# Attention over a pooled grid, then a mixture of adapters: the hidden activations made transposed, gates sent through DRAM, and a new run-out

## The chip, the cores and the metric

The kernel runs on one core of a Trainium2 chip. The core has five engines that this text speaks of: TensorE (PE in the profile, with its weight loads as PEld), VectorE (DVE), ScalarE (ACT), GpSimd (POOL) and SyncE (SP), which only issues transfers here. Transfers run on 16 DMA engines that all queues share. The metric is the device time of one execution in microseconds (us); the time of a kernel is the median of several runs.

## The reference

Four batches of 12,288 queries with 128 channels attend to keys and values that come from a grid, and each attended row then goes through the two best of eight small adapters.

```python
# attention; B, C, H, W = 4, 128, 384, 32, q has H*W rows a batch
kv_pool = kv.reshape(B, H // r, r, W // r, r, C).mean(axis=(2, 4))     # r = 4: 768 keys a batch
k = v = kv_pool.reshape(B, -1, C) @ w_sr
s = (q @ k.transpose(0, 2, 1)) / sqrt(C)
x = softmax(s) @ v                                                     # 49152 x 128 in all
# adapters: E = 8, rank 16
logits = x @ w_gate
top two of the eight logits, w = softmax over these two
delta = sum over the two of  w * ((x @ A[e]) @ B[e])
out = x + delta
```

## The kernel before

The 49,152 rows are worked in 96 chunks (NCH) of 512 rows (NTOK), 24 chunks to a batch. A chunk is four blocks (NS) of 128 rows. Two chunks form a pair, which shares the tiles of the gates.

A chunk c passes these steps, each named by its function:

- `scores(c, r)`, three times: two matmuls of 512 columns give the scores of 256 keys, and ScalarE's exponential writes them as `tt` (lines 284 and 285).
- `weigh(c, h)`, two halves: 24 matmuls with `tt` as weights give the attended rows, their gate logits and the sum of the exponentials, in the two banks `xps` (line 297).
- `normalise(c)`: VectorE's reciprocal, one multiply into `xn`, and four searches for the largest logits (lines 304, 308, 315).
- `gate(p)` and `gate_weights(p)`, once a pair: four small operations on GpSimd, a tanh on ScalarE, two more on GpSimd; the result `gw` has rows on partitions and, for each block, eight gates (lines 324 to 335).
- `transposed(cx, ch)`: TensorE turns the four blocks of `xn` of one chunk and the four blocks of `hg` of an older one into one bank, `t_ps` (line 352), and VectorE copies both out at once (line 361).
- `down(c)`: four matmuls of 128 columns with the transposed x as weights give h, rows on partitions (line 375). `apply_gate(c)`: VectorE multiplies h by the gates, spread over the 16 columns of each expert, into `hg` (line 380).
- `up(c)`: four matmuls with the transposed `hg` as weights give the adapters' sum (line 400). `give(c)`: VectorE adds `xn` (line 407), and SP sends 256 KB out (line 413).

The order of the work on every engine is the order of the program: it is written out by hand (`manual_schedule`), and each engine takes its own instructions in that order. The loop at line 551 works on several chunks in one iteration c: the scores of chunks c + 1 and c + 2, weigh and normalise of c - 1, the transposes of x of c - 2 and hg of c - 4, down and gate of c - 3, up and output of c - 6. On TensorE one iteration reads: scores, first half of weigh, scores, up, second half of weigh, transposes, scores, down.

TensorE's results stand in banks: two tiles of two banks for scores (`ps_s`), two banks for `xps`, one for `t_ps`, and one (`ps_h`, tag `hd`) that h and the adapters' sum use in turn. A step that writes a bank waits until the bank's last reader is done.

SP's transfers are issued in program order too, and a transfer that waits holds up those behind it. On SP stand the rows of kv for later batches (`load_row`, line 85, 512 KB each, planned by chunk in `plan`), the transposing loads of q (`load_q`, line 274, every fourth iteration, from a half-precision copy in DRAM that GpSimd's queue makes, `cast_q`, line 95), and the outputs. All are hardware-issued on one queue, which the profile calls q1; GpSimd's are on q0.

After the loop comes a run-out (lines 604 to 664): the last two chunks' weigh and everything that is left of the last six chunks, in an order of its own, with the scores' banks given back and used as single banks (`bank`, `fbank`). There `give` has two other forms: ScalarE copies and GpSimd adds, and two outputs leave on ScalarE's queue. At the end a flag (`bad`) decides whether a slow exact branch runs; it does not run here.

## Time and profile before

| | |
|---|---|
| time, median of 3 runs | 395.42 us (394.81 to 395.48) |
| profiled execution, its own time | 395.21 us |
| its span, first to last instruction | 393.4 us |
| granted TensorE clock, mean | 0.997 |
| busy: PE, DVE, ACT, POOL | 377.9, 323.4, 305.9, 206.9 us |
| transfers | 76.47 MB, 194 GB/s in the mean |

The page of a profile gives each engine's busy time and the chain of work that ended last, followed back from the last instruction, by engine and line. A group row reads: line, engine, operation, output and inputs, shapes, count, then busy time, mean duration of one, and the idle time of the engine before it with what ended that. A row of the timeline reads: start and length in us, engine, line, operation, and how many were merged. A row of stretches gives, for each engine, busy time and instructions, then the granted clock, the DMA engines' busy share and GB/s. Matmuls are pipelined, so their durations overlap, and the distance between starts is what one costs.

### The profile page before, as it was taken

What the parts mean: (1) busy time and instruction counts of PE and PEld (TensorE: products, weight loads), DVE (VectorE), ACT (ScalarE), POOL (GpSimd) and SP (SyncE); (2) the same over time, 40 slices, a digit from 0 to 9 for tenths busy, and PEclk for the clock granted to TensorE, in tenths of its full rate; (3) what the DMA queues carried; (4) which work ended last, traced back from release to release, by engine and by line L of the source; (5) the groups of instructions that cost most, each with busy time, mean ns of one, the idle gap of its engine ahead of it and who ended that gap; (6) DMA issues with size and microseconds to landing.
All of it is one profiled execution on the core that took longest, in us unless ns stands there. A gap on an engine that the chain in (4) does not pass through costs nothing.

```text
span 393.4 us, 11525 instructions
## 1 busy us (share of the span) xinstructions
PE 377.9 (96%) x4589; PEld 301.2 (77%) x4589; DVE 323.4 (82%) x911; ACT 305.9 (78%) x387; POOL 206.9 (53%) x389
## 2 busy tenths in 40 slices
PE   4989999999999999999999999999999999999993
PEld 1457768888887887888878888888788888878882
DVE  3776777888888889888888888888888888888984
ACT  1558888878888888887877888888878877877863
POOL 1011598895688666563487666573442332322353
PEclk9999999999999999999999999999999999999998
DMA  8989997998898899298997998275678583222124
GB/s 255 393 279 167 358 262 229 275 218 218 258 211 234 256 164 266 83 211 246 238 238 225 241 237 211 92 166 130 135 92 205 136 188 102 88 82 83 55 86 160
DMA packets 69784, 76.47 MB, mean 194 GB/s; under 512 B 49664, under 2 KB 49920, under 8 KB 69376
## 3 DMA queue, kind: packets, MB, share of 16 engines
q1 hardware_dynamic: 67264, 63.45, 55.8%
q0 software_dynamic: 704, 11.54, 16.9%
q10 hardware_dynamic: 1760, 0.73, 0.7%
q8 instruction: 36, 0.59, 0.6%
q14 instruction: 20, 0.16, 0.1%
HBM read 50.53 MB, written 36.70 MB: 222 GB/s over the span
## 4 chain that ended last, share of the span: by engine, by line
PE 93%; ACT 2%; DMA 1%; POOL 1%; DVE 1%; issue 0%; ACTq 0%; POOLq 0%
PE xps L297 34%; PE sg L284 31%; PE t_ps L352 11%; PE d_ps L400 5%; PE h_ps L375 5%; PE w_ps L495 2%; PE v_ps L173 1%; DMA w_gate_sb<-in_moe_w_gate_dram 1%; ACT tt L285 1%; PE k_ps L198 1%; PE kp_ps L165 1%; ACT qT L481 0%; PE t_ps L477 0%; ACT xh L359 0%; POOL osb L411 0%
## 5 line engine op out<-in xcount | busy, mean ns | idle before, releaser
L285 ACT ACTIVATE tt<-sg 128x1024 f16<-128x1024 f32 x288 | 281.3, 1024 | 57.2 <-PE sg L284 56.8
L284 PE MATMUL sg<-qT,kfT 128*128 128x512 f16 x576 | 171.0, 379 | 1.3 <-ACT tt L285 1.0
L297 PEld LDWEIGHTS <-tt 128*128 128x128 f16 x2304 | 152.6, 112 | 22.1 <-DVE xn L308 0.7
L297 PE MATMUL xps<-vext,tt 128*128 128x137 f16 x2304 | 169.4, 223 | 0.0
L407 DVE TENSOR_TENSOR osb<-d_ps,xn 128x512 f32<-128x512 f32 x90 | 62.3, 692 | 35.3 <-PE d_ps L400 35.2
L324 POOL TENSOR_TENSOR arg<-xn,top 128x64 f32<-128x64 f32 x47 | 14.9, 317 | 121.6 <-DVE top L315 116.5
L308 DVE TENSOR_TENSOR xn<-xps,rinv_all 128x548 f32<-128x548 f32 x96 | 70.0, 729 | 3.3
L380 DVE TENSOR_TENSOR hg<-h_ps,gw 128x512 bf16<-128x512 f32 x93 | 63.2, 679 | 2.4 <-PE h_ps L375 2.4
L149 POOL TENSOR_TENSOR kvt<-kvt 128x1024 f32<-128x1024 f32 x27 | 63.9, 2368 | 1.3 <-PE sg L284 1.1
L361 DVE COPY xh<-t_ps 128x1024 bf16<-128x1024 bf16 (+1 forms) x93 | 62.5, 672 | 0.0
L284 PEld LDWEIGHTS <-kfT 128*128 128x128 f16 x576 | 45.0, 98 | 3.6 <-issue 2.1
L375 PEld LDWEIGHTS <-xh 128*128 128x128 bf16 x384 | 29.3, 98 | 21.5
L400 PEld LDWEIGHTS <-xh 128*128 128x128 bf16 x384 | 29.1, 98 | 21.5 <-ACT xh L359 0.6
L315 DVE MAX8 top<-xn 128x8 f32<-128x8 f32 x384 | 35.9, 156 | 3.3
L352 PE MATMUL t_ps<-id_bf,hg 128*128 128x128 bf16 x376 | 36.3, 219 | 0.5 <-ACT xh L359 0.5
L352 PE MATMUL t_ps<-id_bf,xn 128*128 128x128 bf16 x376 | 36.3, 219 | 0.0
L400 PE MATMUL d_ps<-b_bf,xh 128*128 128x128 bf16 x368 | 35.6, 219 | 0.5 <-ACT xh L359 0.5
L375 PE MATMUL h_ps<-a_bf,xh 128*128 128x128 bf16 x372 | 35.9, 219 | 0.0
L352 PEld LDWEIGHTS <-xn 128*128 128x128 bf16 x384 | 26.4, 98 | 0.7 <-DVE xn L308 0.4
L352 PEld LDWEIGHTS <-hg 128*128 128x128 bf16 x384 | 25.3, 98 | 0.9 <-DVE hg L380 0.8
L334 POOL TENSOR_SCALAR th<-th 128x64 f32<-128x64 f32 x48 | 18.0, 375 | 13.7 <-ACT th L332 13.5
L304 DVE RECIPROCAL rinv_all<-xps 128x4 f32<-128x4 f32 x96 | 17.5, 183 | 7.5 <-PE xps L297 5.0
(112 smaller groups left out, 240.2 us busy)
## 6 DMA issues: line engine op xcount, KB each, us to landing
kvt<-in_kv_dram SPq DMA_DIRECT2D x48, 512.0 KB, 6.1
out_dram<-osb SPq DMA_DIRECT2D x94, 256.0 KB, 3.0
q_h<-in_q_dram POOLq DMA_DIRECT2D x22, 512.0 KB, 7.1
q<-in_q_dram SPq DMA_DIRECT2D x2, 1024.0 KB, 9.9
out_dram<-osb ACTq DMA_DIRECT2D x2, 256.0 KB, 3.5
qT<-q_h SPq DMA_TRANSPOSE x22, 8.4
w_in<-in_w_sr_dram ACTq DMA_DIRECT2D x1, 64.0 KB, 1.8
a_f<-in_moe_A_dram ACTq DMA_DIRECT2D x1, 64.0 KB, 10.5
```

The costliest lines, as they stand in the source:

```text
L149: eng.tensor_tensor(v[:, 0], v[:, 0], v[:, d], op=ALU.add)
L284: mm(sg[:, k], kfT[b][:, j * P:(j + 1) * P], qc, start=True, stop=True)
L285: nc.scalar.activation(tt[c][:, 2 * r:2 * r + 2], sg, AF.Exp, bias=0.0, scale=scale)
L297: mm(o, tt[c][:, j, rows], vext[b][:, j, 0:VW], start=(j == 0 and s % 2 == 0), stop=(j == NJ - 1 and s % 2 == 1), skip_group_check=True)
L308: nc.vector.tensor_tensor(xn[c].rearrange("p (b s) v -> p b s v", b=2), xv, ri.rearrange("p (b s) -> p b s", b=2).unsqueeze(3).broadcast_t ...
L315: nc.vector.max(gin[c // 2][:, (c % 2) * NS + s], xn[c][:, s, C:C + E])
L352: mm(t_ps[:, k, s], src, id_bf, is_transpose=True, start=(i == 0), stop=(i == len(todo) - 1), skip_group_check=True)
L361: nc.vector.tensor_copy(xh[:, lo:hi_], t_ps[:, lo:hi_])
L375: mm(hps[c][:, s], xT[c][:, s], a_bf, start=(s == 0), stop=(s == NS - 1))
L380: nc.vector.tensor_tensor(hg[c].rearrange("p s (e r) -> p (s e) r", r=RK), hps[c].rearrange("p s (e r) -> p (s e) r", r=RK), g.rearrange(" ...
L400: mm(dps[c][:, s], hgT[c][:, s], b_bf, start=(s == 0 and fresh), stop=(s == NS - 1), skip_group_check=True)
L407: nc.vector.tensor_tensor(osb, dps[c], xn[c][:, :, 0:C], op=ALU.add)
```

## The change

Four things change.

1. **h is made transposed.** In the loop, `gated_hidden(c)` takes `a_bf` as the weights and the transposed x of a chunk as 512 moving columns: one matmul gives h with the adapters' columns on partitions. VectorE multiplies it by gates of the same layout, and the result is already what `up` wants as weights. So `hg` is not transposed for these chunks.
2. **The gates come transposed over DRAM.** `gw` is now in half precision. Once a pair, TensorE transposes it (64 rows of 128) into the bank `t_ps`; VectorE copies it out, SP stores it in DRAM (`g_h`, 16 KB), and `load_gates` reads it back so that each expert's row stands on its 16 partitions (256 KB in SBUF). This holds for the first 90 chunks (`OWN`); the last six keep the old way.
3. **The lags change.** gated_hidden works on chunk c - 6, up and output on c - 7. The evacuations of x and of the gates are separate copies, the output has 6 buffers instead of 8.
4. **The run-out is new.** Banks are taken and given back in another order, ScalarE copies most results out (`take`), GpSimd adds four of them, all outputs leave on SP, and the last chunk is worked in two halves. The check that sets `bad` comes last.

Beside these, the last two kv rows are loaded as two halves each, and the four `kpT` tiles are slices of one, which saves three transfers in the branch that does not run.

```diff
+    g_h = qdram.tile([NCH // 2, E, 2 * NS, P], F16, name="g_h")
...
-        gw[p] = small.tile([P, 2 * NS, E], FP32, tag="gw", name="gw")
+        gw[p] = small.tile([P, 2 * NS, E], F16, tag="gw", name="gw")
...
+    def transposed(cx, cg=NCH, p=NCH):
+        t_ps = ps_t.tile([P, 2, NS, P], BF16, tag="tp", name="t_ps")
+        hi = xn[cx].bitcast(U16)[:, :, 1:2 * C:2].bitcast(BF16)
+        more = chunk_ok(cg) or p < NCH
+        for s in range(NS):
+            mm(t_ps[:, 0, s], hi[:, s], id_bf, is_transpose=True,
+               start=(s == 0), stop=(s == NS - 1 and not more), skip_group_check=True)
+
+        def second():
+            if chunk_ok(cg):
+                for s in range(NS):
+                    mm(t_ps[:, 1, s], hg[cg][:, s], id_bf, is_transpose=True,
+                       start=False, stop=(s == NS - 1), skip_group_check=True)
+            elif p < NCH:
+                mm(t_ps[0:2 * NS * E, 1, 0].bitcast(F16), gw[p].rearrange("p s e -> p (s e)"),
+                   id_h, is_transpose=True, start=False, stop=True, skip_group_check=True)
 
         def evacuate(act=False):
...
+            if p < NCH:
+                g_sb = small.tile([2 * NS * E, P], F16, tag="gt", name="g_sb")
+                copy(g_sb, t_ps[0:2 * NS * E, 1, 0].bitcast(F16))
+                nc.sync.dma_start(g_h[p].rearrange("e s t -> s e t"), g_sb)
+            xT[cx] = run.tile([P, NS, P], BF16, tag="xt", name="xt", bufs=5)
+            copy(xT[cx], t_ps[:, 0])
...
+    def load_gates(p):
+        gE[p] = run.tile([P, 2 * NS, P], F16, tag="ge", name="ge", bufs=3)
+        nc.sync.dma_start(
+            gE[p].rearrange("p s t -> p (s t)"),
+            g_h[p].rearrange("e s t -> e (s t)").unsqueeze(1).broadcast_to([E, RK, 2 * NS * P]))
+
+    def gated_hidden(c):
+        h_ps = mtile([P, NS, P], name="h_ps")
+        mm(h_ps, a_bf, xT[c], start=True, stop=True)
+        hgT[c] = run.tile([P, NS, P], BF16, tag="ht", name="ht", bufs=3)
+        nc.vector.tensor_tensor(hgT[c], h_ps, gE[c // 2][:, (c % 2) * NS:(c % 2 + 1) * NS],
+                                op=ALU.mult)
...
         weigh(c - 1, 0)
+        if c == NCH - 2:
+            down(c - 4, stile("h_ps")[:, 0])
+            apply_gate(c - 4)
         next_scores()
-        if chunk_ok(c - 6):
-            up(c - 6)
-            give(c - 6)
+        if chunk_ok(c - 7):
+            up(c - 7)
+            give(c - 7)
+        if c % 2 == 0 and 0 <= (c - 4) // 2 < OWN // 2:
+            load_gates((c - 4) // 2)
         weigh(c - 1, 1)
...
-        evacuate = transposed(c - 2, c - 4)
+        pair = (c - 3) // 2
+        second, evacuate = transposed(
+            c - 2, c - 4 if c - 4 >= OWN else NCH, pair if c % 2 and 0 <= pair < OWN // 2 else NCH)
         next_scores()
...
-        if chunk_ok(c - 3):
-            down(c - 3)
+        if chunk_ok(c - 6):
+            gated_hidden(c - 6)
+        second()
+        if c == NCH - 2:
+            down(c - 3, stile("h_ps")[:, 0])
             apply_gate(c - 3)
         evacuate(c == NCH - 2)
...
     gate_weights(q_ - 1, nc.gpsimd)
+    y4 = ps_x.tile([P, 2, 512], FP32, tag="x", name="y4")
+    weigh(n - 1, 0, y4)
+    gated_hidden(n - 6)
+    up(n - 7, bank(0))
+    give(n - 7)
     weigh(n - 1, 1)
...
+    turn(high(n), 0, NS, bank(0), xT, n)
+    gate_args(n, 0, NS, nc.vector, top5, arg5, msk5)
+    gate_tanh(0, NS, arg5)
...
+    for c, o in ((n - 6, o6), (n - 5, o0), (n - 4, o1), (n - 3, o2)):
+        add(c, o, nc.gpsimd)
+        put(c, o)
+        if c == n - 4:
+            put(n - 2, o3)
     tail_ok()
...
+    up(n - 1, mtile([P, NTOK], name="d4"))
+    give(n - 1)
...
+    put(n, o5)
+    all_ok(bank(1))
```

Here `take(c)` is ScalarE's copy of the adapters' sum, `add` the addition of `xn` in place, `put` the output's transfer, `turn` a transpose with its evacuation, and n is the last chunk, 95.

More of the change, by code (lines that the diff above doesn't have):

```diff
@@ new lines, in turn @@
+    def turn(src, lo, hi, bank_, store, key, act=True):
+        t_ps = bank_.bitcast(BF16)[:, 0:(hi - lo) * P].rearrange("p (s c) -> p s c", c=P)
+        for s in range(lo, hi):
+            mm(t_ps[:, s - lo], src[:, s], id_bf, is_transpose=True,
+               start=(s == lo), stop=(s == hi - 1), skip_group_check=True)
+        if key not in store:
+            x_or_h = ("xt", 5) if store is xT else ("ht", 3)
+            store[key] = run.tile([P, NS, P], BF16, tag=x_or_h[0], name="xr", bufs=x_or_h[1])
+        if act:
+            nc.scalar.activation(store[key][:, lo:hi], t_ps, AF.Copy)
+        else:
+            nc.vector.tensor_copy(store[key][:, lo:hi], t_ps)
@@ new lines, in high, with hidden @@
+    def high(c):
+        return xn[c].bitcast(U16)[:, :, 1:2 * C:2].bitcast(BF16)
+    def hidden(c, lo, hi, bank_):
+        hb = as_tokens(bank_)[:, 0:hi - lo]
+        for s in range(lo, hi):
+            mm(hb[:, s - lo], xT[c][:, s], a_bf, start=(s == lo), stop=(s == hi - 1))
+        return hb
+    n = NCH - 1
+    q_ = n // 2
+    top = small.tile([P, 2 * NS, 8], FP32, tag="top", name="top")
+    top4, top5 = top[:, 0:NS], top[:, NS:2 * NS]
+    pair = xpool.tile([P, 2 * NS, VW], FP32, tag="xn", name="xn")
```

223 lines of the change are left out of this document (133 added, 90 removed).

## The prediction

> **What bounds the kernel now.** I read the page first: busy shares, then the chain that ended last, which names the engine whose time is the kernel's time.
>
> ```profile
> PE 377.9 (96%) x4589; PEld 301.2 (77%) x4589; DVE 323.4 (82%) x911; ACT 305.9 (78%) x387; POOL 206.9 (53%) x389
> ...
> PE 93%; ACT 2%; DMA 1%; POOL 1%; DVE 1%; issue 0%; ACTq 0%; POOLq 0%
> PE xps L297 34%; PE sg L284 31%; PE t_ps L352 11%; PE d_ps L400 5%; PE h_ps L375 5%; PE w_ps L495 2%; PE v_ps L173 1%; DMA w_gate_sb<-in_moe_w_gate_dram 1%; ACT tt L285 1%; PE k_ps L198 1%; PE kp_ps L165 1%; ACT qT L481 0%; PE t_ps L477 0%; ACT xh L359 0%; POOL osb L411 0%
> ```
>
> The chain is TensorE for 93% of the span, and transposes (L352) are 11% of it. Next the groups by line and shape, and then one iteration of the loop in order of time, TensorE and then VectorE.
>
> ```profile
> L352 PE MATMUL t_ps<-id_bf,hg 128*128 128x128 bf16 x376 | 36.3, 219 | 0.5 <-ACT xh L359 0.5
> L361 DVE COPY xh<-t_ps 128x512 bf16<-128x512 bf16 x3 | 1.2, 415 | 0.0
> L409 ACT ACTIVATE osb<-d_ps 128x512 f32<-128x512 f32 x2 | 1.2, 597 | 0.6 <-PE d_ps L400 0.6
> ```
>
> ```profile
> 203.55 0.39 PE L352 MATMUL t_ps<-id_bf,xn 128*128 128x128 bf16 x4
> 203.77 0.39 PE L352 MATMUL t_ps<-id_bf,hg 128*128 128x128 bf16 x4
> 204.00 0.59 PE L284 MATMUL sg<-qT,kfT 128*128 128x512 f16 x2
> 204.43 0.39 PE L375 MATMUL h_ps<-a_bf,xh 128*128 128x128 bf16 x4
> 204.65 0.59 PE L284 MATMUL sg<-qT,kfT 128*128 128x512 f16 x2
> ...
> 206.24 0.39 PE L400 MATMUL d_ps<-b_bf,xh 128*128 128x128 bf16 x4
> 206.46 0.88 PE L297 MATMUL xps<-vext,tt 128*128 128x137 f16 x12
> 207.18 0.39 PE L352 MATMUL t_ps<-id_bf,xn 128*128 128x128 bf16 x4
> ```
>
> ```profile
> 203.75 0.18 DVE L304 RECIPROCAL rinv_all<-xps 128x4 f32<-128x4 f32 x1
> 203.97 0.73 DVE L308 TENSOR_TENSOR xn<-xps,rinv_all 128x548 f32<-128x548 f32 x1
> 204.73 0.37 DVE L315 MAX8 top<-xn 128x8 f32<-128x8 f32 x4
> 205.03 0.67 DVE L380 TENSOR_TENSOR hg<-h_ps,gw 128x512 bf16<-128x512 f32 x1
> 205.61 0.68 DVE L361 COPY xh<-t_ps 128x1024 bf16<-128x1024 bf16 x1
> 206.66 0.69 DVE L407 TENSOR_TENSOR osb<-d_ps,xn 128x512 f32<-128x512 f32 x1 [0.37 <-PE d_ps L400]
> ```
>
> Starts, not durations, give the price on TensorE, since its matmuls overlap. One iteration is 207.18 - 203.55 = 3.63 us; one starts with the scores at 204.65, so the others at 201.02 and 211.91. The four transposes of hg take 204.00 - 203.77 = 0.23 (0.056 each), one 512-column matmul (204.43 - 204.00) / 2 = 0.215, the four of h_ps 204.65 - 204.43 = 0.22. VectorE works 3.32 us of the 3.63.
>
> **The change, part by part.** *Transposes of hg* go for 90 of the 96 chunks (the last six keep the old way): 90 x 0.225 = 20.2 us. *h as one 512-column matmul* instead of four of 128: 0.215 against 0.22, nothing. *A transpose of the gates* for each of 45 pairs, with 128 moving columns: 45 x 0.056 = 2.5 us. TensorE's balance is -17.7 us, all on the chain, if nothing else becomes late. The iteration falls to about 3.43 us.
>
> *VectorE.* The evacuation shrinks from 0.68 to 0.415 (the 128x512 row); the multiply by gates keeps its size (0.67); a copy of 64x128 gates comes every second iteration, at most the 0.42 of the 128x512 row. The sum is 0.18 + 0.73 + 0.37 + 0.67 + 0.42 + 0.21 + 0.69 = 3.27, under 3.43. *ScalarE* needs three exponentials and half a tanh:
>
> ```profile
> 201.00 1.94 ACT L285 ACTIVATE tt<-sg 128x1024 f16<-128x1024 f32 x2 [0.74 <-PE sg L284]
> 202.83 0.26 ACT L332 ACTIVATE th<-arg 128x64 f32<-128x64 f32 x1
> 203.63 0.32 POOL L335 TENSOR_TENSOR gw<-th,msk 128x64 f32<-128x64 f32 x1
> ```
>
> 3 x 0.97 + 0.13 = 3.0, also under. The gate transpose runs where h_ps ended (204.65 here) and POOL's gw is ready at 203.95: TensorE does not wait for it. The banks of xps come free later relative to need: normalise ends at 204.70 and the next weigh starts at 204.65 + 0.43 = 205.08; this slack of 0.38 falls by the 0.2 saved, to 0.15 or so, still positive. These parts I cost at nothing; if a cover is gone, each lost 0.1 us costs 9 us over 92 iterations.
>
> *The way over DRAM.* The path is: copy of gates to SBUF at an odd iteration's end, store, load behind it on SP, multiply in the iteration after next. The load cannot be issued before the store has landed, and in every second pair it stands on SP behind a transposing load of q (L274) and an output.
>
> ```profile
> kvt<-in_kv_dram SPq DMA_DIRECT2D x30, 512.0 KB, 5.5
> out_dram<-osb SPq DMA_DIRECT2D x50, 256.0 KB, 4.9
> ...
> qT<-q_h SPq DMA_TRANSPOSE x13, 8.8
> ```
>
> ```profile
> DMA to landing us min/median/max: 5.0/8.8/12.2
> ```
>
> ```profile
> DMA to landing us min/median/max: 3.8/8.1/9.9
> ```
>
> The issue table of 47 to 235 us, and the landing times of q's transposing loads there and (7 loads) from 235 to 345 us. SP's own rows:
>
> ```profile
> 48.55 1.86 SPq L274 DMA_TRANSPOSE qT<-q_h  x1
> ...
> 212.69 4.38 SPq L274 DMA_TRANSPOSE qT<-q_h  x1
> 217.16 1.65 SPq L413 DMA_DIRECT2D out_dram<-osb  x2
> ...
> 227.27 3.05 SPq L274 DMA_TRANSPOSE qT<-q_h  x1
> ```
>
> The price of one 256 KB transfer in the DMA engines' time comes from the quiet stretch 335 to 373 us, where only ten outputs run (second column of the queue row MB, third share of 38 us):
>
> ```profile
> q1 hardware_dynamic: 1516, 2.75, 18.8%
> ...
> out_dram<-osb SPq DMA_DIRECT2D x10, 256.0 KB, 2.0
> ```
>
> 0.188 x 38 / 10 = 0.71 us. A gate load moves as many bytes, so 0.71 is its lower bound; the upper is 1.42, that of an input row of 512 KB at this rate, because reads from DRAM land slower than writes (kv 5.5 against 4.9 us median). I take 0.71, as it has the output's bytes. The store (16 KB) counts 0.1.
>
> The budget from the start S of an iteration with a q load: two periods, then 205.03 - 201.02 = 4.0 us into the third until VectorE multiplies, then 0.3 us of slack until the next up needs the result (now 206.24 - 205.70 = 0.54, less the 0.2 saved). With key and value work the period up to 230 us is (227.27 - 48.55) / 48 - 0.2 = 3.52, later 3.43. So 11.3 and 11.15 us. Spent of it: q's load starts 0.8 after S (212.69 against 211.91); now the gate store stands ahead of it on SP, ready only 1.5 after S (VectorE's multiply ends 4.7 after the iteration before began, 0.2 for the copy, less 3.43), which I cost at nothing where the load is late, because there the queue is full anyway (4.38 us to issue one), and at 1.1 us more at the upper end. Output and gate load follow at 0.71 each. The gates are late when q's load takes over 11.3 - 0.8 - 1.4 = 9.1 us (8.95 later). Spreading the upper half of the landings evenly, 8.8 to 12.2: mean excess 3.1² / 2 / 3.4 = 1.41, times 6.5 loads = 9.2 us. Later, 8.1 to 9.9: 0.95² / 2 / 1.8 = 0.25, times 3.5 = 0.9. A late multiply holds VectorE and then TensorE's up, so it is lost in full: +10.1 us. With 1.1 us more spent the first half gives some 20, the second 4: upper end +24. The lower end is 0, if the queue drains better.
>
> *SP and POOL.* Stores and loads are 90 more issues on SP, which waits for the store's landing with outputs and kv rows queued behind it; outputs have 6 buffers, 20 us of cover. POOL loses nothing in the loop. The split of two kv rows is two more issues of 0.5 us, hidden; kp_keep works in the untaken branch only.
>
> *The run-out.* It carries more: up is one chunk later, h three chunks, so 0.22 x 3 of TensorE work moves behind the loop, and ScalarE evacuates 12 times 0.6 us after weigh of chunk 94. Against that the last transfer no longer leaves on ACT's queue:
>
> ```profile
> 377.51 1.60 PE L297 MATMUL xps<-vext,tt 128*128 128x137 f16 x24
> ...
> 387.79 0.69 DVE L407 TENSOR_TENSOR osb<-d_ps,xn 128x512 f32<-128x512 f32 x1 [0.17 <-PE d_ps L400]
> ```
>
> ```profile
> out_dram<-osb ACTq DMA_DIRECT2D x2, 256.0 KB, 3.5
> ```
>
> From that weigh's end (379.1) to the span's end, 393.4, is 14.3 us now: the last addition ends at 388.5, its output lands 3.5 later and 1.4 more pass. In the new order ScalarE is what I find last: 0.6 until its first copy, 8.3 of copies and tanh in one row, 1.6 for the final up and addition, an output from SP at the 2.0 us of the quiet stretch, and the 1.4: 13.9. With the 0.6 that the loop hands over, net +0.2, counted as 0, bounds -1.5 to +1.5.
>
> **Sum.** Profiled run 395.2 (span 393.4 + 1.8 around it): 395.2 - 17.7 + 10.1 + 0 = 387.6. The median of the runs is 0.2 above: 387.8.
>
> **The rivals.**
> *A, no lateness.* Landings shrink because DMA has idle time after 235 us. 395.4 - 17.7 = 377.7. For it: half the landings are already short enough; against: 9 us is passed often.
>
> *B, slower: the DMA engines become the bound up to 235 us.*
>
> ```profile
> 47.00:108.00 61.00, 60.03 (x745) 48.34 (x743) 49.94 (x143) 50.53 (x66) 48.61 (x74) 1.00 0.93 249
> 108.00:171.00 63.00, 63.00 (x796) 51.25 (x795) 54.09 (x152) 51.95 (x65) 46.28 (x71) 1.00 0.84 205
> 171.00:235.00 64.00, 64.00 (x806) 51.93 (x805) 55.19 (x161) 52.74 (x67) 38.83 (x73) 1.00 0.94 233
> ```
>
> The column before the last is the DMA share: 0.93 x 61 + 0.84 x 63 + 0.94 x 64 = 169.8 us of 188. The faster loop would have 188 - 50 x 0.2 = 178 for it, and 25 pairs come on top. At 1.42 + 0.1 each that is 38, so 208 us of work: the stretch lasts 208, and 395.4 - 17.7 + 30 = 408. It decides once a pair costs over (178 + 17.7 - 169.8) / 25 = 1.04 us; at 0.81 it gives 390. That point lies 0.23 above my price and 0.48 below the upper one, and outputs that land at 4.9 us in this stretch against 2.0 in the quiet one show how much queue there is already; but a share that counts overlapping packets twice overstates the work. So a third of the chance.
>
> The Trainium skill, "DMA: Bandwidth & Descriptors", section "Why a DMA increments its semaphore by 16 and not by 1", says that a transfer is spread over the largest number of engines, up to 16, that divides the outermost dimension of both sides. The gate load's source has 8 experts outermost, so by that rule 8 engines carry it at twice the time, and B's upper price would hold: 408 by it, 388 by mine. The trace of before has no transfer of that shape and cannot show it.
>
> *C, some wait eats the gain without DMA* (VectorE or the xps banks, 0.19 us in each of 92 iterations): 395.4 - 17.7 + 17.5 = 395.2. Against it: VectorE's 0.37 us of idle.
>
> **How the numbers follow.** Forecast 0.36 (382 to 394), A 0.23, B 0.34, C 0.07. About 0.2% is what a measurement can tell from no change, 394.6 to 396.2. Faster 0.36 + 0.23 + 0.02 = 0.61, same 0.05, slower 0.34. The forecast is the likeliest, 387.8; the 8 in 10 range goes from A to just short of B's upper price, 378 to 405.
>
> **What would show it.** Right: L352 loses the hg group, TensorE idles before up (L400), released by VectorE's hgT multiply that itself waits for the DMA of the gates, mostly in iterations with a q load before 235 us; a period of about 3.43 elsewhere. A: no such wait. B: the wait comes in nearly every pair before 235 us and the DMA share there is near 1. Wrong in another way: a wait of TensorE for normalise, or a run-out more than 1.5 us longer.

## The result, and the profile after

The changed kernel takes 454.0 us (median of four executions, 448.1 to 461.3) against 395.1 us: a ratio of 1.144, with an interval of 1.133 to 1.155. The prediction was 387.8 us, with a range of 378 to 405. It missed both the sign and the range. An execution over 1.5% above the quickest of its kernel counts as slow: one of these four (461.3 us, which the ratio leaves out), three of the four each of e7, e11, e13 and e16, and the profiled ones of e4, e8, e9, e11, e13 and e16.

The page of the changed kernel, its busy line, two rows of the slices and the chain:

```profile
PE 389.3 (86%) x4008; PEld 277.4 (61%) x4008; DVE 308.4 (68%) x957; ACT 311.9 (69%) x393; POOL 206.3 (46%) x393
...
PEclk9999988997999699899989789999999999999998
DMA  8989797967979989869889967986798696532314
...
PE 55%; DMA 30%; DVE 7%; SPq 3%; issue 2%; ACT 1%; DVEq 0%
PE xps L306 21%; PE sg L293 19%; DMA ge<-g_h 15%; DMA g_h<-g_sb 13%; PE d_ps L432 4%; PE t_ps L353 3%; PE h_ps L396 3%; SPq L93 2%; DVE ht L398 2%; DMA kvt<-in_kv_dram 2%; DVE xn L317 1%; PE t_ps L362 1%; PE v_ps L182 1%; SPq L451 1%; PE w_ps L536 1%
```

TensorE has 581 instructions fewer than before, and the chain has left it: 55% instead of 93%. The two transfers of the gates are 28% of the chain, the load (ge<-g_h) 15% and the store in front of it (g_h<-g_sb) 13%. The list of waits (total, times, longest) says who stood for them, first the engines, then SP's queue:

```profile
DVE ht L398 <- DMA ge<-g_h: 58.3, 22, 11.6
PE d_ps L432 <- DVE ht L398: 47.1, 18, 11.3
```

```profile
SPq L389 <- DMA g_h<-g_sb: 66.9, 22, 8.1
```

VectorE waits 58.3 us for gates, TensorE's `up` then waits 47.1 us for VectorE, and the load itself stands on SP, 22 times, until the store has landed, 66.9 us in all. The stretches, in the columns of the prediction (the last three are clock, DMA share, GB/s):

```profile
47.00:108.00 61.00, 42.93 (x396) 28.97 (x394) 29.73 (x94) 33.16 (x41) 38.38 (x48) 0.89 0.85 214
108.00:171.00 63.00, 54.83 (x579) 39.46 (x578) 42.11 (x134) 44.60 (x57) 36.14 (x63) 0.95 0.87 211
171.00:235.00 64.00, 58.36 (x608) 42.23 (x606) 45.44 (x146) 46.84 (x60) 30.98 (x58) 0.95 0.87 215
```

Before, the same stretches had DMA shares of 0.93, 0.84 and 0.94. With 45 more stores and 45 more loads on the queue, two of the three are lower, so by this share the DMA engines are not the bound (a kernel that runs late also asks for its transfers later). One wait for gates, rows of VectorE, TensorE and SP in order of time, with rows between them left out:

```profile
149.20 0.69 DVE L398 TENSOR_TENSOR ht<-h_ps,ge 128x512 bf16<-128x512 f32 x1 [7.26 <-DMA ge<-g_h]
149.95 0.61 PE L432 MATMUL d_ps<-b_bf,ht 128*128 128x128 bf16 x4 [6.94 <-DVE ht L398]
150.35 1.59 PE L306 MATMUL xps<-vext,tt 128*128 128x137 f16 x12
151.04 0.60 SPq L389 DMA_DIRECT2D ge<-g_h  x1
```

Behind a wait of 7 us, twelve matmuls of `weigh` take 1.59 us where the rows of before had 0.88. This long wait is paid a second time: the granted clock is 0.50 from 149.95 to 153.60 us, and such places pull the clocks of the stretches down to 0.89 and 0.95. (The Trainium skill, "TensorE: Matmul & The Clock Gate", Part 1, says that an idle window of about 3.4 us brings the clock to half; the trace agrees on the half, 0.50 behind a wait of 6.94 us, and these rows don't show how long the window is.)

The landing times follow from the semaphore updates in the trace. These are the transfers that belong to the wait at 149.20:

```
issue    queue  transfer          landed   after
132.27   SP     store of gates    140.48    8.2
132.98   SP     transposing q     146.64   13.7
133.77   POOL   cast of q         146.40   12.6
140.50   SP     load of gates     149.11    8.6     issued 0.02 after the store landed
```

8.2 and 8.6 us, one after the other. The multiply was due at 141.9. Counted in the same way over the pairs up to 240 us, a store takes 5.5 us to land in the median and the load behind it 4.7; from 383 us on, where little else moves, 1.8 and 3.6. The longest wait of all, 11.6 us, has another shape: its store landed after 4.2 us, SP was then busy for 3.4 us more with the issue of an output, and the load took 13.9 us. In both places a transposing load of q and a cast of q move at the same time, and these land after 13.7 and 12.6 us in the first, 18.4 and 17.1 in the second (before, the longest q load took 12.2). No run changes that overlap, so its share is open.

### The profile page after: what moved, and what is told of

It is laid out like the page before. It is cut to its first block, busy times and chain, and to the rows that moved or that the text cites. A ratio compares the mean times of both kernels' runs of the same rounds, so it can differ in the third digit from the quotient of the medians.

```text
span 452.5 us, 10659 instructions
## 1 busy us (share of the span) xinstructions
PE 389.3 (86%) x4008; PEld 277.4 (61%) x4008; DVE 308.4 (68%) x957; ACT 311.9 (69%) x393; POOL 206.3 (46%) x393
## 4 chain that ended last, share of the span: by engine, by line
PE 55%; DMA 30%; DVE 7%; SPq 3%; issue 2%; ACT 1%; DVEq 0%
PE xps L306 21%; PE sg L293 19%; DMA ge<-g_h 15%; DMA g_h<-g_sb 13%; PE d_ps L432 4%; PE t_ps L353 3%; PE h_ps L396 3%; SPq L93 2%; DVE ht L398 2%; DMA kvt<-in_kv_dram 2%; DVE xn L317 1%; PE t_ps L362 1%; PE v_ps L182 1%; SPq L451 1%; PE w_ps L536 1%
## 5 line engine op out<-in xcount | busy, mean ns | idle before, releaser
L294 ACT ACTIVATE tt<-sg 128x1024 f16<-128x1024 f32 x288 | 285.7, 1025 | 99.6 <-PE sg L293 98.9
L293 PE MATMUL sg<-qT,kfT 128*128 128x512 f16 x576 | 175.9, 389 | 1.4 <-ACT tt L294 1.0
L398 DVE TENSOR_TENSOR ht<-h_ps,ge 128x512 bf16<-128x512 f32 x90 | 61.3, 681 | 60.0 <-DMA ge<-g_h 58.3
L432 PE MATMUL d_ps<-b_bf,ht 128*128 128x128 bf16 x352 | 35.2, 224 | 47.2 <-DVE ht L398 47.1
L432 PEld LDWEIGHTS <-ht 128*128 128x128 bf16 x368 | 26.5, 99 | 74.8 <-DVE ht L398 59.8
L293 PEld LDWEIGHTS <-kfT 128*128 128x128 f16 x576 | 46.0, 99 | 18.4 <-issue 2.2
L370 DVE COPY xt<-t_ps 128x512 bf16<-128x512 bf16 x92 | 37.8, 411 | 0.0
L396 PE MATMUL h_ps<-xt,a_bf 128*128 128x512 bf16 x90 | 35.4, 393 | 0.3 <-DVE osb L446 0.2
L336 POOL TENSOR_SCALAR msk<-msk 128x64 f32<-128x64 f32 x47 | 17.5, 373 | 4.2
L362 PEld LDWEIGHTS <-gw 128*64 128x64 f16 x45 | 4.9, 108 | 21.5 <-issue 18.4
L344 POOL TENSOR_TENSOR gw<-th,msk 128x64 f16<-128x64 f32 x47 | 15.1, 322 | 3.9
```

The costliest lines, as they stand in the source:

```text
L293: mm(sg[:, k], kfT[b][:, j * P:(j + 1) * P], qc, start=True, stop=True)
L294: nc.scalar.activation(tt[c][:, 2 * r:2 * r + 2], sg, AF.Exp, bias=0.0, scale=scale)
L370: nc.vector.tensor_copy(dst, src)
L396: mm(h_ps, a_bf, xT[c], start=True, stop=True)
L398: nc.vector.tensor_tensor(hgT[c], h_ps, gE[c // 2][:, (c % 2) * NS:(c % 2 + 1) * NS], op=ALU.mult)
L432: mm(dps[c][:, s], hgT[c][:, s], b_bf, start=(s == 0 and fresh), stop=(s == NS - 1), skip_group_check=True)
```

## The experiments

Times in us below are medians. Where differences are worked out, each kernel stands as its ratio times 395.4.

**Without the transfers (e1).** Is the whole loss the gates' way over DRAM?

```diff
-                nc.sync.dma_start(g_h[p].rearrange("e s t -> s e t"), g_sb)
...
-        gE[p] = run.tile([P, 2 * NS, P], F16, tag="ge", name="ge", bufs=3)
-        nc.sync.dma_start(gE[p]..., g_h[p]...)
+        gE[p] = g_one                     # a constant tile
```

> The changed kernel without the store and the load of the gates: every chunk of the loop is multiplied by a constant 0.5 instead of its gates, so the output is not the reference's; all other work, the gates' transpose and copy too, stays. If the whole loss comes with these transfers, the 17.7 us of TensorE come out: 376 to 380 us, a granted clock near 1. If the loop or the run-out lost time by themselves (VectorE, the banks of xps), it stays above 390.

393.1, ratio 0.995 [0.991, 0.999]. The transfers cost some 59 us. But 393 is far above the 377.7 that the prediction gives without lateness: something else in the loop or the run-out is dearer than I had it. (The constant makes the output another than the reference's.)

**What the gate transpose costs (e5).** In e1's steady part the iterations take 3.40 and 3.68 us in turn, and only the second kind has the gate transpose. TensorE's rows in e1 around one, and the group of its weight loads:

```profile
203.32 0.38 PE L394 MATMUL h_ps<-xt,a_bf 128*128 128x512 bf16 x1
203.63 0.24 PE L364 MATMUL t_ps<-id_h,gw 128*64 128x128 f16 x1
203.81 0.60 PE L295 MATMUL sg<-qT,kfT 128*128 128x512 f16 x2
...
L364 PEld LDWEIGHTS <-gw 128*64 128x64 f16 x45 | 4.8, 106 | 21.6 <-issue 15.2 <-POOL gw L346 5.5 <-POOL sq L228 0.8
```

From h_ps to the scores is 0.49 us, where 0.215 for h_ps and 0.056 for the transpose make 0.27. The difference is around the load of weights, 64 columns wide where all others in the loop are 128. The experiment pads it with zeros:

```diff
-        gw[p] = small.tile([P, 2 * NS, E], F16, tag="gw", name="gw")
+        gw[p] = gws[p % 3][:, 0:2 * NS]          # gws: [P, 4 * NS, E], set to zero once
...
-                mm(t_ps[0:2 * NS * E, 1, 0].bitcast(F16), gw[p].rearrange("p s e -> p (s e)"),
+                mm(t_ps[:, 1, 0].bitcast(F16), gws[p % 3].rearrange("p s e -> p (s e)"),
```

> The kernel of e1 (no gates sent or fetched, the multiplication by a constant, so the output is not the reference's), with one thing changed: the gates stand in a block of 128 columns of which 64 are zero, so that the gate transpose on TensorE loads 128 columns of weights as its neighbours do, and not 64. In e1 the iterations without the gate transpose take 3.40 us and those with it 3.68 us, 0.28 us for one transpose where I had put 0.056 us. Theory narrow: it is the load of 64 columns that is not hidden behind the matmuls before it (its row shows 0.34 us of idle time per load, its neighbours 0.07 us or less); then the odd iterations fall to 3.46 us, 45 x 0.22 = 9.9 us go, and the kernel takes about 383 us (380 to 386). Theory wait: what costs is that the transpose waits for GpSimd's product, or that it stands by itself in the middle of other work; then the odd iterations stay at 3.6 to 3.7 us and the time at 392 to 394 us. The Trainium skill, TensorE: Matmul & The Clock Gate, section Weight-path perf modes, says that the fast weight load is taken when the number of weights is 128 and the type is not FP32; it speaks for the first theory.

383.7, ratio 0.969 [0.967, 0.972], 10 us less than e1 for a wider block of zeros. The same place in e5:

```profile
199.65 0.38 PE L398 MATMUL h_ps<-xt,a_bf 128*128 128x512 bf16 x1
199.86 0.22 PE L368 MATMUL t_ps<-id_h,gws 128*128 128x128 f16 x1
199.92 0.59 PE L299 MATMUL sg<-qT,kfT 128*128 128x512 f16 x2
```

0.27 us: the transpose costs 0.06 as predicted, once its weights are 128 wide. The trace agrees with the rule of the Trainium skill ("TensorE: Matmul & The Clock Gate", "Weight-path perf modes") that the expectation names, as far as the time goes: 0.28 us with 64 columns, 0.06 with 128.

**The load without the store's wait (e2).** The same bytes move, but the load reads a constant, the same 16 KB each time (and the output is another), and so waits for no store.

```diff
-            g_h[p].rearrange("e s t -> e (s t)")...
+            g_c[0].rearrange("e s t -> e (s t)")...      # written once, at the start
```

> The same stores and loads, but the loads read a constant that was stored once at the start, so no load waits for a store; the output is not the reference's, because the gates are constant. Theory 1 (two landings in a row: a store that lands behind rows of kv, and a load that SP holds until then): 380 to 400 us, and TensorE's wait for the gates falls from some 60 us to under 20. Theory 2 (the gate transfers take so much of the DMA engines that everything is late): above 430 us, since all the traffic is still there.

428.2, ratio 1.083 [1.074, 1.091]. Waiting for the store is worth some 24 us; 35 remain without it.

```profile
DVE ht L402 <- DMA ge<-g_c: 29.6, 13, 8.3
```

VectorE still waits, for loads that wait for nobody. The DMA shares of the three stretches are 1.02, 0.87 and 0.88 here, hardly above the changed kernel's in the last two, though SP stands for no store.

**The traffic by itself (e7), and over 16 engines (e12).** e7 is e2 with a product that reads a constant tile: the loads run and nobody wants them. e12 moves the same bytes in another order. (Both have two buffers for the gates instead of three.)

```diff
# e7, against e2
-        nc.vector.tensor_tensor(hgT[c], h_ps, gE[c // 2][...], op=ALU.mult)
+        nc.vector.tensor_tensor(hgT[c], h_ps, g_two[...], op=ALU.mult)
# e12, against e7: rank outermost in the load, one run per row in the store
-            g_c[0].rearrange("e s t -> e (s t)").unsqueeze(1).broadcast_to([E, RK, 2 * NS * P]))
+            g_c[0].rearrange("e s t -> e (s t)").unsqueeze(0).broadcast_to([RK, E, 2 * NS * P]))
-                nc.sync.dma_start(g_h[p].rearrange("e s t -> s e t"), g_sb)
+                nc.sync.dma_start(g_h[p].rearrange("e s t -> (e s) t"), g_sb)
```

> The traffic of e2 (a store and a broadcast load per pair, the load from a constant that is written once, so that it waits for no store), but the multiplication reads a constant tile: nobody waits for the loads any more, and the output is not the reference's. e1 without traffic took 393.1 us, e2 with it 428.2 us, of which 29.6 us was VectorE waiting for gates. Theory lateness: the traffic costs only where VectorE waits for it; then this is near e1, 393 to 398 us. Theory contention: the traffic slows the rows of kv, the casts and q's loads, and the loop then waits for these; then it stays near e2, 420 to 430 us, with the waits moved to sums of kv or scores. Between them, both have a share.

> e7 (traffic that nobody waits for, product with a constant, output not the reference's) with the same bytes moved in a form that spreads over 16 DMA engines: rank outermost in the load, one run per row in the store. e7 took 410.6 us, without traffic 393.1 us. Theory bytes: the 17.5 us are the 11.8 MB through engines that are full anyway; then 405 to 412 us. Theory half: each transfer keeps 8 engines for twice as long while the others run dry; then about half of the 17.5 us goes, 397 to 404 us.

e7: 410.6, ratio 1.037 [1.030, 1.045]. e12: 397.2, ratio 0.998 [0.993, 1.002]. Against e1 the traffic costs 16.7 us by the ratios in the shape that the changed kernel gives it, and 1 us by the ratios (4 by the medians) when 16 rows stand outermost instead of 8. But e7's four executions lie between 401.7 and 423.2, and the quickest, which is the profiled one, is only 9 us above the quickest of e1 and of e12 (392.3 and 392.6). So the price of this shape is 9 to 17 us. The first stretch of e7, then of e12:

```profile
47.00:108.00 61.00, 56.05 (x596) 41.22 (x596) 42.29 (x135) 47.51 (x61) 45.55 (x67) 0.97 1.09 223
```

```profile
47.00:108.00 61.00, 59.97 (x654) 44.04 (x654) 46.14 (x151) 52.73 (x67) 49.03 (x74) 1.00 1.04 272
```

The share is above 1 in both, so it counts overlapping packets twice; but e12 moves 272 GB/s here and e7 223. In the next two stretches the two are alike (255 and 246 for e7, 254 and 257 for e12). That half of the engines carry a gate transfer is also to be read from the changed kernel's semaphores: one of them counts 451 updates for 33 transfers of which 11 are of gates, and 22 x 16 + 11 x 9 = 451, so 16 for an ordinary transfer and 9 for one of gates. By the section of the Trainium skill that the prediction cites ("DMA: Bandwidth & Descriptors", "Why a DMA increments its semaphore by 16 and not by 1"), the issuer writes what the engines in use leave of 16 at once; 8 engines and that one write would be the 9. In e12 the same count comes out with 16 for every transfer of the gates in the loop.

**The order on SP's queue (e3), 16 engines (e4), both (e6).** The real kernel again.

```diff
# e3: the store goes ahead of kv's rows, the gate load ahead of q's load
+        if cs < NCH and cs % GRP == 0 and cs // GRP + 2 < NQ:
+            load_q(cs // GRP + 2)                 # moved from the iteration's start to behind load_gates
...
         evacuate(c == NCH - 2)
+        prep_loads(c)                             # the kv rows, moved from before the store
# e4: store and load as in e12; A's, B's and the gates' columns in the order (rank, expert)
```

> The changed kernel with another order on SP alone: in an iteration the gate store goes ahead of the rows of kv, and the gate load goes ahead of the transposing load of q. Theory 1: the store lands after about 2 us and the load after about 4, within the budget of some 7 to 11 us: 378 to 390 us. Theory 2: the same work for the engines, above 430 us.

> The changed kernel with the adapters' columns in another order (rank outermost, expert inside) and the gates stored expert by expert, so that the outermost dimension of the load is 16 and that of the store 64. By the Trainium skill, DMA: Bandwidth & Descriptors, section Why a DMA increments its semaphore by 16 and not by 1, both then run on 16 engines instead of 8, and the landing of a load falls from 3.5 to about 2.8 us. Theory 1: the waits for earlier transfers stay, so 435 to 450 us. Theory 2 (saturated engines, by the doubled load on half of them): the larger part of the loss goes, 385 to 410 us.

> The edits of e3 (store ahead of kv's rows and load ahead of q's load on SP's queue) and of e4 (the load taken rank outermost, the store in one run per row, so that both go over 16 engines and not 8) together; the result is the reference's. e3 took 437.8 us and e4 443.2 us against 454.0 us. If each takes away a part of the same latency (store behind rows; load on half of the engines), the gains add: 454.0 - 16.3 - 10.9 = 427 us, 422 to 432. If what bounds is the sum of the traffic and SP's queue standing until the store has landed, neither edit reaches it and it stays at 435 to 440 us.

e3: 437.8, ratio 1.107 [1.101, 1.113]. e4: 443.2, from two executions of 437.7 and 448.7. e6: 430.7, ratio 1.082 [1.071, 1.092]. As far as two executions of e4 can tell, the gains add (427 by the sum), but most of the loss is untouched. SP in e3:

```profile
SPq L391 <- DMA g_h<-g_sb: 68.1, 34, 7.4
```

With the store early, SP stands as long as in the changed kernel, 34 times instead of 22.

**More time for the gates (e8, e9, e13).**

```diff
# e8: gated_hidden on c - 8, up on c - 9; four late iterations bring it back to c - 6
-        if chunk_ok(c - 6):
-            gated_hidden(c - 6)
+        for x in due.get(c, ()):
+            gated_hidden(x)
# e9: also the load one iteration later, and gates padded as in e5
# e13: e8, with e6's order and 16 engines, and padded
```

> The changed kernel with the gated product and the projection up of a chunk put two iterations later (8 and 9 iterations behind instead of 6 and 7; back to 6 and 7 in the last iterations), so that the gates have about 7 us more to arrive; one more buffer for the transposed x, one less for output rows; stores, loads and their order on SP's queue are as in the changed kernel, and the result is the reference's. Theory lateness: nearly all of the 61 us beyond e1 is gates that come a few us too late; a store took 5 to 9 us to land and the load behind it 4 to 9 us, 10 to 17 us together where 11 us were there; with 18 us there, the time is 393 to 402 us. Theory contention: the DMA engines can't move more, and the gates fall behind whatever slack they have; then 425 to 455 us. Theory holding: SP's queue stands until the store lands, and q's loads and kv's rows behind it come late: then VectorE's wait for gates is nearly gone, and TensorE waits for q or GpSimd for kv instead, 405 to 430 us.

> e8 with two more changes: the load is issued one iteration later, when the store has mostly landed, so that SP's queue is held less, and the gates are padded to 128 columns as in e5. The result is the reference's. If lateness and the narrow weight load are the whole loss, this is e5's time and a few us for the traffic: 383 to 390 us, below the kernel before (395.1 us). If holding of SP's queue was a share, e9 gains more over e8 than e5 over e1 (more than 10 us). If the traffic itself is the bound, 415 us or more.

> e6 (order on SP's queue, 16 engines) with the two further iterations of e8 before the gates are needed and the gates padded to 128 columns as in e5. The result is the reference's. e6 took 430.7 us, with 31.9 us of VectorE waiting for gates and SP standing 65.5 us for stores to land; e12 shows that the traffic in this form costs about 4 us when nobody waits; e5 that the padding gives 9.4 us. Theory lateness: with 7 us more nobody waits, and this is 393.1 - 9.4 + 4 = 388 us, up to 398. Theory holding: SP stands for each store whatever the slack, kv's rows and q's loads behind it are issued late, the DMA engines run dry meanwhile, and the first 240 us are longer: 405 to 422 us, with VectorE's wait for gates nearly gone.

e8: 430.5, ratio 1.077 [1.069, 1.086]. e9: 429.3, ratio 1.073 [1.067, 1.079]. e13: 424.1, between the theory of holding (405 to 422) and e6; its quickest execution, 415.3, is within that range, but the theory wanted VectorE's wait nearly gone, and it is 23.2. These three carry a cost of their own, which I had not seen: of the iterations that make up the lag, two take 6.1 us, some 5 us in all (e17 shows why). Even without these, 7 us more for each pair did not make the gates be in time. Nor did e9 gain the 10 us and more on e8 that its expectation asks for if standing counts: it gained 1.2, and so not even the 10 us that the padding gives without transfers. e8's waits, VectorE's and SP's, and e13's:

```profile
DVE ht L398 <- DMA ge<-g_h: 22.8, 11, 5.2
```

```profile
SPq L389 <- DMA g_h<-g_sb: 92.7, 22, 8.4
```

```profile
DVE ht L407 <- DMA ge<-g_h: 23.2, 13, 4.5
```

```profile
SPq L398 <- DMA g_h<-g_sb: 91.2, 43, 7.0
```

VectorE's wait falls from 58 to 23 us in these two, and SP's grows from 67 to over 90 (in e9 they are 38.0 and 70.5). What the slack buys, the queue gives away: up to 240 us a store leaves SP 8.7 us after VectorE's copy of the gates in the median of e8 and 8.4 in e13, where it was 1.5 in the changed kernel. That this backlog comes from SP's standing isn't shown: in e7, where SP stands for no store, it is 7.5.

**Standing alone (e16).** e1 with the store put back and a load of 2 KB that has to wait for it; nobody reads what it loads.

```diff
+                nc.sync.dma_start(g_h[p].rearrange("e s t -> s e t"), g_sb)
...
+        nc.sync.dma_start(gl, g_h[p][:, 0])
```

> e1 (product with a constant, output not the reference's) with the store of each pair's gates put back, and behind it on SP's queue, at the gate load's place, a load of 2 KB in place of 256 KB that has to wait for the store's landing; nobody reads what it loads. So there is almost no traffic and nobody who waits for gates: only SP's queue stands until each store has landed. e1 took 393.1 us. Theory holding: kv's rows, q's loads and output rows behind it are issued late while the DMA engines run dry; then 403 us or more. Theory lateness alone: 393 to 396 us.

404.4, but its four executions are 393.8, 402.5, 406.2 and 409.5. By the quickest, standing costs nothing (e1: 393.1); why the other three are longer isn't shown. In the profiled one, of 406.2 us, the list of waits from 236 to 266 us has the outputs, for which the prediction had "20 us of cover":

```profile
DVE osb L447 <- DMA out_dram<-osb: 9.2, 2, 7.9
```

All six output buffers were taken, and VectorE, then TensorE, stood 7.9 us for one to land. That output was ready at 231.3, left SP at 248.7 and landed 12.1 us later, again beside a load and a cast of q, of 15.0 and 13.8 us; from 236 to 262 us SP stood for a store once, for 3.6 us. So the theory of holding is neither shown nor excluded by e16.

**Another queue (e11).** e8 with store and load issued by GpSimd.

```diff
-                nc.sync.dma_start(g_h[p].rearrange("e s t -> s e t"), g_sb)
+                nc.gpsimd.dma_start(g_h[p].rearrange("e s t -> s e t"), g_sb)
# and the same in load_gates
```

> e8 (gates needed two iterations later) with the store and the load on GpSimd's queue in place of SP's, so that kv's rows, q's loads and output rows wait for no gates. The result is the reference's. If SP's queue standing until the store lands is the greater part of what e8 (430.5 us) has over e7 (410.6 us, the same traffic, nobody waits), this falls to 408 to 418 us. If GpSimd, which now stands until the store lands, delays its sums of kv or the gates' own products, the waits of kv's sums and of POOL grow and it stays at 425 us or more.

494.2, the slowest of all. The wait moved with the load:

```profile
POOL ge L389 <- DMA g_h<-g_sb: 118.0, 42, 12.4
```

GpSimd makes the gates themselves and the sums of kv; while it stands, the next pair's gates are not made.

**The run-out by itself (e14).** Chunks 0 to 87 the old way, one pair by gates, the new run-out.

```diff
+        if 0 <= c - 3 < X:            # X = 88; gates padded
+            down(c - 3)
+            apply_gate(c - 3)
```

> The kernel before's way for chunks 0 to 87, one pair (88 and 89) by gates over DRAM, and the changed run-out: the price of the run-out by itself. The result is the reference's. In e1 the last four chunks' reciprocals stand 10.9 us apart where before had 8.3 us, and from the last of them to the end it is 11.6 us for 11.9 us: if the run-out carries that with it, 395.4 + 2.3 = 397.7 us (396.5 to 399). My prediction had it at 0, within 1.5 us: 394 to 397 us. If it is an effect of what the changed loop leaves behind, 395.4 us.

398.3, ratio 1.008 [1.005, 1.011]: the run-out costs 3.1 us. The reciprocals of the last four chunks, in the kernel before and in e14:

```profile
373.20 0.18 DVE L304 RECIPROCAL rinv_all<-xps 128x4 f32<-128x4 f32 x1
376.63 0.18 DVE L304 RECIPROCAL rinv_all<-xps 128x4 f32<-128x4 f32 x1
379.21 0.18 DVE L304 RECIPROCAL rinv_all<-xps 128x4 f32<-128x4 f32 x1 [0.64 <-PE xps L297]
381.51 0.17 DVE L304 RECIPROCAL rinv_all<-xps 128x4 f32<-128x4 f32 x1
```

```profile
373.35 0.18 DVE L317 RECIPROCAL rinv_all<-xps 128x4 f32<-128x4 f32 x1
376.56 0.18 DVE L317 RECIPROCAL rinv_all<-xps 128x4 f32<-128x4 f32 x1
380.29 0.18 DVE L740 RECIPROCAL rinv_all<-y 128x4 f32<-128x4 f32 x1
383.73 0.18 DVE L740 RECIPROCAL rinv_all<-y 128x4 f32<-128x4 f32 x1
```

Level at chunk 92, 2.2 us behind at chunk 95; from there to the span's end both take 11.9 us. The old run-out brought the last two chunks at 2.6 and 2.3 us, the new one at 3.7 and 3.4.

**The new way only where there is room (e10, e15, e17, e18).** The old way for chunks 0 to 55, the gates over DRAM, padded, from chunk 56 on, when the last kv rows have been asked for.

```diff
# e10: X = 56 in the diff of e14, gates padded
# e15: e10 with the order and the 16 engines of e6
# e17: e10 with e8's two further iterations
# e18: e17 with the doubled steps of its four catch-up iterations set apart
```

> The kernel before's way (product with tokens in rows, four transposes of it) for chunks 0 to 55, and the changed way with gates padded to 128 columns for chunks 56 to 89, that is, after the last row of kv has been asked for; the changed run-out. The result is the reference's. If the transfers cost time only where the DMA engines are full, they are hidden here: 34 iterations at 3.43 us (mean of 3.40 and 3.45) in place of 3.63 us are 6.8 us, and the run-out gives 2.5 us: 395.4 - 9.3 = 386 us (383 to 389), better than both kernels. If gates come late in the quiet part too, 395 us or more.

> e10 (the changed way only from chunk 56 on, gates padded) with the edits of e6: gate store and gate load ahead of kv's rows and of q's load on SP's queue, and the load over 16 engines. The result is the reference's. In e10 the iterations from 56 on stood at 3.40 and 3.45 us but for some of 3.9 to 4.5 us, where SP had stood 4.2 to 4.7 us at a q load that waits for its buffer and the gate load behind it was issued as much later. If that is all that was lost there, this takes 395.4 - 6.8 + 2.3 (the run-out, as read from e1) = 391 us (389 to 393), faster than both kernels; otherwise it stays at e10's 395 to 398 us.

> e10 (the changed way only from chunk 56 on, gates padded to 128 columns) with the gates needed two iterations later, as in e8, so that a gate load that is issued 4 to 5 us late, behind a q load for which SP stands, is still in time. The result is the reference's. By 34 iterations at 3.43 us in place of 3.63 us (6.8 us) and the run-out's price as e14 shows it (2.5 us) this is 395.4 - 6.8 + 2.5 = 391 us (389.5 to 393), faster than both kernels. If lateness in the quiet part is not what e10 lost, 395 to 398 us.

> e17 with the second product and the second projection of the four catch-up iterations (86 to 89) moved between the two halves of the work around them, so that they do not follow one another on one PSUM bank; nothing else. The result is the reference's. In e17 chunk 80 stood 4.3 us earlier than in the kernel before, and then two iterations took 6.1 us each, with TensorE waiting 1.16 us for VectorE's product and 0.78 us for its sum between two uses of that bank. Without these waits 4 to 5 us go: 392 to 394 us, faster than the kernel before by 0.5 to 1%. If the time is lost elsewhere, it stays at 397 us.

e10: 398.3, ratio 1.004 [1.000, 1.009]; here I had taken the run-out for a gain of 2.5 us, having read e1's reciprocals the wrong way round. e15: 405.9, ratio 1.027 [1.022, 1.033]; it loses before any gates are sent, chunk 56 comes at 245.4 us instead of 240.9. Its order of kv and q is one possible cause; another is the order of the columns, with which the old way's multiply by the gates takes 1.08 us instead of e10's 0.68, 58 times. No run separates them. e17: 398.2, ratio 1.006 [1.002, 1.010]: chunk 80 comes at 325.4 us against 329.7, so with room and slack the loop is as fast as predicted, 3.40 and 3.45 us; then the catch-up gives it back:

```profile
352.60 0.38 PE L400 MATMUL h_ps<-xt,a_bf 128*128 128x512 bf16 x1
354.13 0.38 PE L400 MATMUL h_ps<-xt,a_bf 128*128 128x512 bf16 x1 [1.16 <-DVE ht L402]
...
357.10 0.38 PE L436 MATMUL d_ps<-b_bf,ht 128*128 128x128 bf16 x4 [0.78 <-DVE osb L450]
```

Two products in a row share the one bank `hd`, and TensorE stands until VectorE has read the first. With these set apart e18 takes 396.6, ratio 1.001 [0.998, 1.004]: level with the kernel before. Its four catch-up iterations still take 4.3 to 4.5 us each, some 4 us more in all than four at 3.40 and 3.45. Its profiled execution is 1.9 us ahead at chunk 92 (371.3 against 373.2) and loses that in the run-out. No version that computes the whole was faster than the kernel before.

## Why the prediction was wrong

Starting from the 377.7 us that its terms give without lateness:

```
                                                    us      from
terms of the prediction without lateness          377.7
run-out, 0 in the prediction                       +3.1     e14 - before
gate transpose, 0.06 in the prediction            +10.2     e1 - e5
traffic, and VectorE waits for loads              +34.6     e2 - e1
the load waits for the store                      +24.3     after - e2
sum                                               449.9     measured 452.4 by the ratio
```

The differences go by one order of taking things away; in another order the last two would share the sum otherwise. Of the 34.6 us the traffic with nobody waiting is 9 to 17, as e7 has it. The 2.5 us between the sum and the measured time are those under "Not resolved".

*Right.* The 0.23 us for four transposes of hg: iterations without a gate transpose take 3.40 us instead of 3.63, so VectorE, ScalarE and the banks of xps made no new wait in them. Late gates hold VectorE and then `up`, as the prediction said under "what would show it"; only it expected this behind q's loads before 235 us, and 19.4 of the 58.3 us came after 240 us.

*The step that failed: "The way over DRAM".* Its budget knew that "the load cannot be issued before the store has landed", but it counted only the engines' time for the transfers (0.71 for output and load each, 0.1 for the store) and set the store's landing at nothing. The two landings, one behind the other, are 8.2 + 8.6 us in the place shown above and 5.5 + 4.7 us in the median up to 240 us, against a budget of 11.3 us from which q's load also comes. I had rows for what a transfer takes to land in this stretch (5.5 us for kv, 4.9 for outputs) and used them only for the upper price and to argue that the queue is full. Two of those in series are 10 us, which leaves nothing of the 11.3 in the pairs with a q load and little in the others. Without the store's landing in front of the load 24.3 us go (e2), without any transfer 59 (e1).

*A second place in the same step, its size open: "SP, which waits for the store's landing with outputs and kv rows queued behind it; outputs have 6 buffers".* It was costed at nothing. For outputs and kv rows that held in the changed kernel: from 40 to 440 us the list of waits has none for an output or for q, and 2.0 us of GpSimd for a kv row, against VectorE's 58.3 for gates. What the queue does hold up is the next store: the first five pairs' stores left SP 4 to 7 us after VectorE's copy, and in e8 and e13 the lag ate the whole slack. How the waits divide between gates that are late by themselves and gates that are late because SP stood, no run separates: e16's quickest execution shows no cost, and e11 took the wait off SP, but put it on an engine that could bear it less.

*Rival B, "the DMA engines become the bound up to 235 us".* Transfers that slow each other are there, and the size was fair: 20 us more than the forecast by the twofold price, 9 to 17 measured with nobody waiting, and nearly all gone in the form over 16 engines (e12). Its sign, a share near 1 up to 235 us, came in e7 and not in the changed kernel. The forecast took 0.71 us for a gate transfer "as it has the output's bytes"; by e7 and e12, which move the same bytes, the outermost dimension counts too. The upper price rested on reads landing slower than writes, "kv 5.5 against 4.9", but a kv row has 512 KB and an output 256, so these two rows don't show that. B was priced as if only the engines' time counted, and the range ended where it did because none of the cases had lateness and contention at once.

*The transpose of the gates.* "45 x 0.056" took the price of 128-column weights for a load of 64 columns. Measured: 0.28. This term by itself turned the 17.7 us of gain into 7.5.

*The run-out.* The bounds of -1.5 to +1.5 were too narrow: +3.1. I had compared how long the copies behind the last `weigh` take, which came out equal (11.9 us both); what grew is the distance between the last chunks, which I had left as it was.

*Not resolved.* e5 is 12.2 us faster than the kernel before, where 17.7 less 3.1 for the run-out make 14.6. Up to chunk 56 it gains 6.3 us over before (234.6 against 240.9), from 56 to 92 another 6.2; the first part has half again as many iterations, and kv's rows arriving there may be why it gains no more.

## What to carry to other kernels

A round trip through DRAM on a busy queue costs two landings in series, read from the transfers' landing times in that stretch, not their share of the engines' time. More slack for the consumer need not repair it: here the stores left the in-order queue later by as much. Before adding a transfer, look at the outermost dimension of its pattern: 8 there instead of 16 cost 9 to 16 us here with nobody waiting for the data. And a price taken from a row holds for that row's shape: a weight load of half the width made the step that it is part of five times as dear.

## What had not been expected of the hardware

- A transpose with 64 columns of weights costs 0.28 us on TensorE's path, with 128 columns 0.06 (3.68 and 3.45 us an iteration, e1 and e5).
- A store of 16 KB and the load of 256 KB behind it landed after 5.5 and 4.7 us in the median on the busy queue, and after 1.8 and 3.6 where little else moved (the changed kernel).
- After a stall of 7 us the next twelve matmuls took 1.59 us instead of 0.88, at a granted clock of 0.50.
